# Chunk-sized loads in order of need, q over 128 partitions, and decay and bias vectors without element-sized transfers, in a linear-attention-then-highway kernel

## The chip, the cores and the metric

The kernel runs on one core of a Trainium2 chip. The core has five engines with queues of their own: TensorE (PE in the profile; its weight loads are PEld), VectorE (DVE), ScalarE (ACT), GpSimd (POOL) and SyncE (SP), and 16 DMA engines between the chip's memory (HBM), the on-chip memory (SBUF, 128 partitions) and back. Matmul results land in PSUM, which DVE and ACT read. The metric is the device time of one execution in microseconds (us); lower is better.

## The reference

For batch 4, 8 heads, 768 tokens and head dimension 64, a decayed linear attention runs over blocks of 64 tokens, and its output, with heads side by side as 512 features of 3072 tokens, goes through one highway layer:

```python
for b in range(nb):
    qb, kb, vb = (q[:, :, sl], k[:, :, sl], v[:, :, sl])
    intra = np.einsum('bhic,bhjc->bhij', qb, kb) * Dmask[None]      # lam ** (i - j), i >= j
    intra = np.einsum('bhij,bhjd->bhid', intra, vb)
    inter = np.einsum('bhid,bhde->bhie', qb * lam_pow[None], kv_state)
    out[:, :, sl] = intra + inter
    kv_state = lam_block * kv_state + np.einsum('bhsd,bhse->bhde', kb * rev_pow[None], vb)
...
H = np.maximum(x @ w_h, 0.0)
T = 1.0 / (1.0 + np.exp(-(x @ w_t + b_t)))
out = T * H + (1.0 - T) * x
```

lam holds one decay per head, b_t one bias per feature.

## The kernel before

**Tiling.** The kernel uses chunks of 128 tokens: 6 per batch, 24 in all, numbered n = 6 b + c. Heads go in four pairs (hp), so that two heads of 64 fill 128 partitions. The decay is split into a factor of the key's position, multiplied into v (scale_v, by pow_k), and one of the query's position, multiplied into the attention's output (by pow_q, in intra). Both come from lam by ln and exp on ACT at the start.

**One chunk.** cast_k and scale_v (POOL) turn the float32 loads of k and v into bf16; trans_k turns the chunk of k on PE, and ACT copies it out of PSUM. scores, inter and intra are the attention's matmuls, state adds to the running k-times-v sum, which ACT copies to SBUF for the next chunk. q is turned likewise: for batch 0 by chunk (load_q0, cast_q0, trans_q0), for batches 1 to 3 by head pair for a whole batch at once (load_q, cast_q, trans_q). There a partition takes J = 8 tokens that follow one another, so that 96 partitions hold the 768 tokens, and eight transposes of 96 columns give one head pair. All transposes use one PSUM buffer (tag "tr").

**The highway layer** goes in groups of four chunks (512 tokens). A unit (g, j) is ffn_h and ffn_t for 128 of the 512 features: four matmuls of 512 columns each, with relu and sigmoid behind. ffn_out adds T * (H - x) to x and turns it back on PE, one chunk at a time; ACT (at the end DVE too) copies it to o_sb, and SP stores it.

**What sets the order.** The schedule is manual: each engine runs its instructions in the order of the program. The main loop runs over i = 0 to 31. Iteration i casts chunk i+3 and one head pair of the next batch's q (c = 0 to 3) on POOL, turns k of chunk i+2, computes scores of chunk i+1 and the rest of chunk i, turns head pair c-1 of the next batch's q (c = 1 to 4), then does one ffn_h, one ffn_out and one ffn_t, where there is one. Units begin at i = 4, stores at i = 8; at i = 24 to 27 only units and stores are left, at i = 28 to 31 only stores.

**Loads.** All loads of q, k and v and all stores are issued by SP, in order. Batch 0 is loaded by chunk (256 KB each of k, q, v; line 61 and line 70); batches 1 to 3 by batch, 1.5 MB each of q (line 66), k and v (line 58), in that order. Batch 1 and 2's loads stand ahead of the first store, batch 3's behind the second. kf, vf and qf have two buffers of a whole batch each. lam is loaded three times by ACT's queue: once whole into every partition (line 76), and twice as every second element (lines 79, 80) for the head pairs; the bias is loaded with one element per partition (line 252). The weights are loaded and cast to bf16 by POOL's queue (lines 269, 270).

Of the kernel before, what the change touches and what calls it, by code (L numbers as in the profile page):

```python
# [16 lines left out]
def kernel(  # L17
# [11 lines left out]
    nc = tc.nc  # L29
    B, H, S, D = q.shape  # L30
    C = 128
    NCH = S // C
    NP = H // 2
    DM = H * D
    KC = DM // 128
    J = 8
    QP = S // J
    PP = C // J
    N = B * NCH
    G = 4  # L40
# [11 lines left out]
    def load_kv(b, what, src, cs=None):  # L52
        store = {"k": kf, "v": vf}[what]
        if b not in store:
            store[b] = load.tile([C, H, NCH, D], F32, tag=what + "f", name=f"{what}f{b}")
        t = store[b]
        if cs is None:
            nc.sync.dma_start(out=t.rearrange("p h c d -> p (h c) d"),
                              in_=src[b].rearrange("h (c p) d -> p (h c) d", p=C))
        else:  # L60
            nc.sync.dma_start(out=t[:, :, cs, :],
                              in_=src[b, :, cs * C:(cs + 1) * C, :].rearrange("h p d -> p h d"))

    def load_q(b):
        qf[b] = load.tile([QP, H, J * D], F32, tag="qf", name=f"qf{b}")
        nc.sync.dma_start(out=qf[b], in_=q[b].rearrange("h (p j) d -> p h (j d)", j=J))

    def load_q0(c):
        q0f[c] = load.tile([C, H, D], F32, tag="q0f", name=f"q0f{c}", bufs=3)
        nc.sync.dma_start(out=q0f[c], in_=q[0, :, c * C:(c + 1) * C, :].rearrange("h p d -> p h d"))  # L70

    load_kv(0, "k", k, 0)
    load_q0(0)
    load_kv(0, "v", v, 0)
# [6 lines left out]
    for c in range(1, 3):  # L81
        load_kv(0, "k", k, c)
        load_q0(c)
        load_kv(0, "v", v, c)
# [16 lines left out]
    nc.scalar.activation(ln_hp, lam_hp, AF.Ln)  # L101
# [22 lines left out]
    def cast_k(n, eng=None):  # L124
        b, c = divmod(n, NCH)
        kb[n] = work.tile([C, H, D], BF16, tag="kb", name="kb", bufs=4)
        (eng or nc.gpsimd).tensor_copy(kb[n], kf[b][:, :, c, :])  # L127

    def scale_v(n):
        b, c = divmod(n, NCH)  # L130
        vs[n] = work.tile([C, H, D], BF16, tag="vs", name="vs", bufs=4)
        nc.gpsimd.tensor_tensor(vs[n], in0=vf[b][:, :, c, :], in1=pow_k[:, :, c, :].to_broadcast([C, H, D]), op=ALU.mult)  # L132
# [4 lines left out]

    def trans_q0(c):
        if 0 not in qT:
            qT[0] = load.tile([128, NP, NCH, J * PP], BF16, tag="qT", name="qT0")  # L140
# [3 lines left out]
        nc.scalar.activation(qT[0][:, :, c, :], tr, AF.Copy)  # L144

    def cast_q(b, hp):
        qb[b, hp] = work.tile([QP, J, 2, D], BF16, tag="qb", name="qb")
        nc.gpsimd.tensor_copy(qb[b, hp].rearrange("p j e d -> p e j d"),  # L148
                              qf[b][:, 2 * hp:2 * hp + 2, :].rearrange("p e (j d) -> p e j d", j=J))

    def trans_q(b, hp):
        if hp == 0:
            qT[b] = load.tile([128, NP, NCH, J * PP], BF16, tag="qT", name=f"qT{b}")
        tr = ps.tile([128, J, QP], BF16, tag="tr", name="tr")
        for j in range(J):
            nc.tensor.transpose(tr[:, j, :], qb[b, hp][:, j], id128[0:QP, 0:QP])  # L156
        nc.scalar.activation(qT[b][:, hp].rearrange("p c (q j) -> p (c q) j", j=J),  # L157
                             tr.rearrange("p j q -> p q j"), AF.Copy)

    def trans_k(n):  # L160
# [6 lines left out]
    def scores(n):  # L167
        b, c = divmod(n, NCH)
        s_ps = ps.tile([C, 2, NP, C], F32, tag="s", name="s_ps")
        for hp in range(NP):  # L170
            for e in range(2):
                r = slice(64 * e, 64 * e + 64)
                nc.tensor.matmul(s_ps[:, e, hp, :], lhsT=kT[n][r, hp, :], rhs=qT[b][r, hp, c, :], start=True, stop=True)  # L173
        masked[n] = work.tile([C, 2, NP, C], BF16, tag="masked", name="masked")
        for e in range(2):
            nc.vector.tensor_tensor(masked[n][:, e], in0=s_ps[:, e],  # L176
                                    in1=tri.to_broadcast([C, NP, C]), op=ALU.mult)

    def inter(n):
        b, c = divmod(n, NCH)  # L180
        o_ps[n] = ps.tile([128, NP, C], F32, tag="o", name="o_ps")
        if c > 0:
            for hp in range(NP):
                nc.tensor.matmul(o_ps[n][:, hp, :], lhsT=s_bd[n % 2][:, hp, :], rhs=qT[b][:, hp, c, :],  # L184
                                 start=(hp == 0), stop=False, skip_group_check=True)

    def intra(n):
# [42 lines left out]
    def ffn_out(n, eng="act"):  # L230
        g, r = divmod(n, G)
        x_ps = ps.tile([C, DM], F32, tag="x", name="x_ps")
        for j in range(NP):
            for i, t in enumerate((xT[g], thmx[g])):
                nc.tensor.matmul(x_ps[:, j * 128:(j + 1) * 128], lhsT=t[:, j, r * C:(r + 1) * C], rhs=id128,  # L235
                                 start=(j == 0 and i == 0), stop=(i == 1), skip_group_check=True)
        o_sb = work.tile([C, DM], F32, tag="o_sb", name="o_sb", bufs=4)
        if eng == "act":
            nc.scalar.activation(o_sb, x_ps, AF.Copy)  # L239
# [13 lines left out]
    for c in range(3, NCH):  # L253
        load_kv(0, "k", k, c)
        load_q0(c)
        load_kv(0, "v", v, c)
# [21 lines left out]
    while i < N or units or outs:  # L278
        b, c = divmod(i, NCH)
        if i + 3 < N:  # L280
            cast_k(i + 3)
            scale_v(i + 3)
        if i + 3 < NCH:
            cast_q0(i + 3)
        if c < NP and b + 1 < B:
            cast_q(b + 1, c)
        if i + 2 < N:
            trans_k(i + 2)
        if i < N:
            inter(i)  # L290
        if i + 1 < N:
            scores(i + 1)
        if i < N:
            intra(i)
            state(i)
        if i + 2 < NCH:
            trans_q0(i + 2)
        if 1 <= c <= NP and b + 1 < B:
            trans_q(b + 1, c - 1)
        unit = units.pop(0) if units else None  # L300
        if unit:
            ffn_h(*unit)
        if outs:
            ffn_out(outs.pop(0), "dve" if i >= N and i % 2 else "act")
        if unit:
            ffn_t(*unit)
            if unit[1] == NP - 1:
                outs += range(unit[0] * G, unit[0] * G + G)
        if i < N and i % G == G - 1:
            units += [(i // G, j) for j in range(NP)]  # L310
        if c == 3 and b + 2 < B:
            load_q(b + 2)
            load_kv(b + 2, "k", k)
# [32 lines left out]
```

## Time and profile before

| what | value |
|---|---|
| median of 3 runs | 161.88 us (161.64 to 163.24) |
| the profiled execution's own time | 161.08 us |
| its span in the profile | 159.3 us |
| PE busy | 105.4 us, 66% |
| ACT, DVE busy | 77.2 us, 48%; 75.5 us, 47% |
| POOL busy | 57.1 us, 36% |
| moved by DMA | 26.41 MB, mean 166 GB/s |
| read from HBM, written to it | 20.98 MB, 6.29 MB |

A profile is of one execution: its span is 1.8 us shorter than that execution's time. "Busy" counts an engine's instructions, "idle before" the gap before an instruction with what ended it (`<-`). In a chain or timeline row the first number is the start in us from the span's beginning and the second the duration; in a row of stages each engine stands with its busy us and, in brackets, its instructions, and behind them the granted TensorE clock (1.00 is full), the mean share of the DMA engines in use and the rate that they moved. That share can pass 1, since packets overlap. Bytes moved are counted as written: the weights count as 1.05 MB although 2.1 MB are read. L148 is line 148 of the kernel before.

### The profile page before, as it was taken

Reading aid. Unit: us, or ns where it says so; the run is one execution under the profiler, and the core shown is the slowest. Engines: PE = TensorE matmul, PEld = TensorE weight load, DVE = VectorE, ACT = ScalarE, POOL = GpSimd, SP = SyncE. Lnnn points to the kernel's source line nnn. Section 1 sums busy time; section 2 is a strip of 40 time slices with the busy share of each in tenths; the row PEclk is TensorE's granted clock in tenths of the full one; section 3 lists DMA queues with packets and bytes.
Section 4 is the critical chain, followed back from the end, with each engine's and each line's share of the span. In section 5 each row is a group of like instructions: output and inputs, shape, how many; then the busy total and the mean of one; then the engine's idle time right before and its main releaser. Section 6 shows DMA issues by size and latency. Waiting matters only on the chain.

```text
span 159.3 us, 2882 instructions
## 1 busy us (share of the span) xinstructions
PE 105.4 (66%) x1127; PEld 69.3 (44%) x1144; DVE 75.5 (47%) x131; ACT 77.2 (48%) x140; POOL 57.1 (36%) x76
## 2 busy tenths in 40 slices
PE   0104661100275689999999989309999999999740
PEld 0103450000154464566666656205666666555440
DVE  4202333000040442998777778017568877856511
ACT  3065861100045448568885766044557676554320
POOL 4017722100594076784394097055244400000000
PEclk9999999999999999999999999955799999999985
DMA  4299999999999999999579999971111212313333
GB/s 88 47 197 222 190 194 234 218 226 222 205 220 219 184 240 214 221 220 218 126 192 229 205 217 198 219 285 48 66 66 66 70 66 88 114 68 132 127 142 132
DMA packets 36126, 26.41 MB, mean 166 GB/s; under 512 B 20496, under 2 KB 30736, under 8 KB 36112
## 3 DMA queue, kind: packets, MB, share of 16 engines
q1 hardware_dynamic: 33840, 25.17, 72.2%
q0 software_dynamic: 1056, 1.05, 3.9%
q8 instruction: 9, 0.15, 0.5%
q10 hardware_dynamic: 1216, 0.01, 0.4%
q14 instruction: 5, 0.04, 0.1%
HBM read 20.98 MB, written 6.29 MB: 171 GB/s over the span
## 4 chain that ended last, share of the span: by engine, by line
PE 45%; issue 18%; DMA 16%; POOL 7%; SPq 5%; ACT 5%; DVE 1%; POOLq 0%; ACTq 0%
PE h_ps L214 11%; PE t_ps L222 10%; DMA qf<-in_q_dram 7%; PE x_ps L235 6%; DMA out_dram<-o_sb 6%; PE o_ps L191 4%; SPq L70 4%; PE s_ps L173 3%; PE tr L156 3%; DMA vf<-in_v_dram 3%; PE kv_ps L205 3%; PE tr L163 3%; PE o_ps L184 2%; POOL vs L132 2%; POOL qb L148 2%
## 5 line engine op out<-in xcount | busy, mean ns | idle before, releaser
L176 DVE TENSOR_TENSOR masked<-s_ps,tri 128x512 bf16<-128x512 f32 x48 | 30.8, 682 | 41.4 <-PE s_ps L173 41.4
L132 POOL TENSOR_TENSOR vs<-vf,pow_k 128x512 bf16<-128x512 f32 x24 | 25.8, 1077 | 43.4 <-DMA vf<-in_v_dram 25.4
L214 PE MATMUL h_ps<-xT,wh 128*128 128x512 bf16 x87 | 25.4, 397 | 0.8 <-issue 0.4
L222 PE MATMUL t_ps<-xT,wt 128*128 128x512 bf16 x88 | 24.9, 396 | 0.3
L228 DVE TENSOR_TENSOR thmx<-t_sb,hmx 128x512 bf16<-128x512 bf16 x24 | 11.6, 484 | 28.3 <-ACT t_sb L225 28.0
L156 PE MATMUL tr<-id,qb 96*128 96x96 bf16 x96 | 7.6, 235 | 23.0 <-POOL qb L148 14.2
L225 ACT ACTIVATE t_sb<-t_ps,bt_col 128x512 bf16<-128x512 f32 x24 | 16.5, 687 | 12.1 <-PE t_ps L222 10.2
L239 ACT ACTIVATE o_sb<-x_ps 128x512 f32<-128x512 f32 x20 | 11.9, 597 | 20.6 <-PE x_ps L235 13.5
L209 ACT ACTIVATE s_bd<-kv_ps 64x256 bf16<-64x256 f32 x40 | 15.1, 377 | 10.9 <-PE kv_ps L205 10.1
L148 POOL CAST qb<-qf 96x1024 bf16<-96x1024 f32 x12 | 12.7, 1059 | 18.4 <-DMA qf<-in_q_dram 18.4
L157 ACT ACTIVATE qT<-tr 128x768 bf16<-128x768 bf16 x12 | 9.7, 810 | 16.3 <-PE tr L156 16.1
L217 DVE SCALAR_TENSOR_TENSOR hmx<-h_ps,xT 128x512 bf16<-128x512 f32 x24 | 16.4, 682 | 2.3 <-PE h_ps L214 2.2
L163 PE MATMUL tr<-id,kb 128*128 128x128 bf16 x96 | 11.0, 248 | 9.6 <-DVE kb L127 5.1
L156 PEld LDWEIGHTS <-qb 96*128 96x128 bf16 x96 | 6.2, 113 | 24.0 <-POOL qb L148 14.6
L127 POOL CAST kb<-kf 128x512 bf16<-128x512 f32 x23 | 14.0, 609 | 7.1 <-PE kv_ps L205 6.9
L196 DVE TENSOR_TENSOR xT<-o_ps,pow_q 128x512 bf16<-128x512 f32 x24 | 16.3, 679 | 0.0
L165 ACT ACTIVATE kT<-tr 128x512 bf16<-128x512 bf16 x24 | 14.1, 589 | 4.0 <-PE tr L163 4.0
L235 PE MATMUL x_ps<-id,xT 128*128 128x128 bf16 x96 | 14.0, 226 | 2.7 <-ACT o_sb L239 1.4
L163 PEld LDWEIGHTS <-kb 128*128 128x128 bf16 x96 | 8.3, 110 | 15.0 <-DVE kb L127 5.1
L235 PE MATMUL x_ps<-id,thmx 128*128 128x128 bf16 x96 | 14.3, 227 | 0.4 <-DVE thmx L228 0.4
L235 PEld LDWEIGHTS <-thmx 128*128 128x128 bf16 x96 | 9.7, 101 | 6.4 <-issue 3.4
L222 PEld LDWEIGHTS <-wt 128*128 128x128 bf16 x96 | 8.9, 102 | 7.6 <-issue 1.7
(41 smaller groups left out, 113.8 us busy)
## 6 DMA issues: line engine op xcount, KB each, us to landing
out_dram<-o_sb SPq DMA_DIRECT2D x24, 256.0 KB, 2.0
qf<-in_q_dram SPq DMA_DIRECT2D x3, 1536.0 KB, 11.3
kf<-in_k_dram SPq DMA_DIRECT2D x6, 256.0 KB, 5.3
q0f<-in_q_dram SPq DMA_DIRECT2D x6, 256.0 KB, 6.6
vf<-in_v_dram SPq DMA_DIRECT2D x6, 256.0 KB, 5.6
wh<-in_moe_w_h_dram POOLq DMA_DIRECT2D x1, 512.0 KB, 6.8
wt<-in_moe_w_t_dram POOLq DMA_DIRECT2D x1, 512.0 KB, 9.3
kf<-in_k_dram SPq DMA_DIRECT2D x3, 0.2 KB, 17.0
```

Of the source, the lines that this page charges most:

```text
L132: nc.gpsimd.tensor_tensor(vs[n], in0=vf[b][:, :, c, :], in1=pow_k[:, :, c, :].to_broadcast([C, H, D]), op=ALU.mult)
L148: nc.gpsimd.tensor_copy(qb[b, hp].rearrange("p j e d -> p e j d"), qf[b][:, 2 * hp:2 * hp + 2, :].rearrange("p e (j d) -> p e j d", j=J))
L156: nc.tensor.transpose(tr[:, j, :], qb[b, hp][:, j], id128[0:QP, 0:QP])
L163: nc.tensor.transpose(tr[:, hp, :], kb[n][:, 2 * hp:2 * hp + 2, :], id128)
L176: nc.vector.tensor_tensor(masked[n][:, e], in0=s_ps[:, e], in1=tri.to_broadcast([C, NP, C]), op=ALU.mult)
L196: nc.vector.tensor_tensor(xT[g][:, :, r * C:(r + 1) * C], in0=o_ps[n], in1=pow_q[:, :, c * C:(c + 1) * C], op=ALU.mult)
L209: nc.scalar.activation(s_bd[(n + 1) % 2][r, :, r], kv_ps[b][r, :, r], AF.Copy)
L214: nc.tensor.matmul(h_ps, lhsT=wh[:, kc, j * 128:(j + 1) * 128], rhs=xT[g][:, kc, :], start=(kc == 0), stop=(kc == KC - 1))
L217: nc.vector.scalar_tensor_tensor(hmx[g, j], in0=h_ps, scalar=0.0, in1=xT[g][:, j, :], op0=ALU.max, op1=ALU.subtract)
L222: nc.tensor.matmul(t_ps, lhsT=wt[:, kc, j * 128:(j + 1) * 128], rhs=xT[g][:, kc, :], start=(kc == 0), stop=(kc == KC - 1))
L225: nc.scalar.activation(t_sb, t_ps, AF.Sigmoid, bias=bt_col[:, j:j + 1])
L235: nc.tensor.matmul(x_ps[:, j * 128:(j + 1) * 128], lhsT=t[:, j, r * C:(r + 1) * C], rhs=id128, start=(j == 0 and i == 0), stop=(i == 1), s ...
```

## The change

k and v are loaded by chunk throughout, into eight buffers each (LA = 8). For batches 1 to 3, q is loaded by head pair (384 KB), into six buffers; a partition takes J = 6 tokens, so that all 128 partitions are used and six transposes of 128 columns make a head pair. One function, loads(n), issues all that belongs to chunk n: k, q of that chunk (batch 0 only), v, and one head pair of the next batch's q (c = 0 to 3). Chunks 0 to 7 are loaded ahead of the loop, and iteration i ends with loads(i + 8). lam is loaded once; its head-pair form is copied on ACT out of the logarithm that is there. The bias is loaded as four rows of 128 and turned by one transpose on PE. o_sb has six buffers in place of four.

```diff
-    J = 8
-    QP = S // J
-    PP = C // J
+    J = S // 128
+    LA = 8
...
+    def load_k(n):
+        b, c = divmod(n, NCH)
+        kf[n] = load.tile([C, H, D], F32, tag="kf", name="kf", bufs=LA)
+        nc.sync.dma_start(out=kf[n], in_=k[b, :, c * C:(c + 1) * C, :].rearrange("h p d -> p h d"))
...
-        qf[b] = load.tile([QP, H, J * D], F32, tag="qf", name=f"qf{b}")
-        nc.sync.dma_start(out=qf[b], in_=q[b].rearrange("h (p j) d -> p h (j d)", j=J))
+    def load_q(b, hp):
+        qf[b, hp] = load.tile([128, 2, J * D], F32, tag="qf", name="qf", bufs=6)
+        nc.sync.dma_start(out=qf[b, hp], in_=q[b, 2 * hp:2 * hp + 2].rearrange("e (p j) d -> p e (j d)", j=J))
...
+    def loads(n):
+        if n >= N:
+            return
+        b, c = divmod(n, NCH)
+        load_k(n)
+        if b == 0:
+            load_q0(c)
+        load_v(n)
+        if c < NP and b + 1 < B:
+            load_q(b + 1, c)
+
     lam_bc = singles.tile([128, H], F32)
     nc.scalar.dma_start(out=lam_bc, in_=lam.partition_broadcast(128))
-    lam_hp = singles.tile([128, NP], F32)
-    lam_v = lam.rearrange("(p two) -> two p", two=2)
-    nc.scalar.dma_start(out=lam_hp[0:64, :], in_=lam_v[0].partition_broadcast(64))
-    nc.scalar.dma_start(out=lam_hp[64:128, :], in_=lam_v[1].partition_broadcast(64))
...
+    bt_r = singles.tile([KC, 128], F32)
+    nc.scalar.dma_start(out=bt_r, in_=moe_b_t.rearrange("(j p) -> j p", p=128))
+    for n in range(4):
+        loads(n)
...
-    nc.scalar.activation(ln_hp, lam_hp, AF.Ln)
+    for e in range(2):
+        r = slice(64 * e, 64 * e + 64)
+        nc.scalar.activation(ln_hp[r, :], ln_bc[r].rearrange("p (hp e) -> p e hp", e=2)[:, e, :], AF.Copy)
...
-        qb[b, hp] = work.tile([QP, J, 2, D], BF16, tag="qb", name="qb")
+        qb[b, hp] = work.tile([128, J, 2, D], BF16, tag="qb", name="qb")
...
-        tr = ps.tile([128, J, QP], BF16, tag="tr", name="tr")
+        tr = ps.tile([128, J, 128], BF16, tag="tr", name="tr")
         for j in range(J):
-            nc.tensor.transpose(tr[:, j, :], qb[b, hp][:, j], id128[0:QP, 0:QP])
+            nc.tensor.transpose(tr[:, j, :], qb[b, hp][:, j], id128)
...
-        o_sb = work.tile([C, DM], F32, tag="o_sb", name="o_sb", bufs=4)
+        o_sb = work.tile([C, DM], F32, tag="o_sb", name="o_sb", bufs=6)
...
     scores(0)
+    id_f = singles.tile([KC, KC], F32)
+    nc.vector.tensor_copy(id_f, id128[0:KC, 0:KC])
+    bt_ps = ps.tile([128, KC], F32, tag="x", name="bt_ps")
+    nc.tensor.transpose(bt_ps, bt_r, id_f)
     bt_col = singles.tile([128, KC], F32)
-    nc.scalar.dma_start(out=bt_col, in_=moe_b_t.rearrange("(j p) -> p j", p=128))
...
-    load_q(1)
-    load_kv(1, "k", k)
-    load_kv(1, "v", v)
+    nc.vector.tensor_copy(bt_col, bt_ps)
+    for n in range(4, LA):
+        loads(n)
...
-        if c == 3 and b + 2 < B:
-            load_q(b + 2)
-            load_kv(b + 2, "k", k)
-            load_kv(b + 2, "v", v)
+        loads(i + LA)
```

SP's queue shows what the loads' new order is. In the kernel before, batch 0's last chunk is followed by the whole of batch 1 and then batch 2 (qf1 is q of batch 1, and so on; the number behind an underscore tells tiles of one name apart):

```order
L70 DMA q0f5_166<-in_q_dram 128x8x64
L61 DMA vf0_73<-in_v_dram 128x8x64
L66 DMA qf1_169<-in_q_dram 96x8x512
L58 DMA kf1_171<-in_k_dram 128x48x64
L58 DMA vf1_173<-in_v_dram 128x48x64
L66 DMA qf2_447<-in_q_dram 96x8x512
```

In the changed kernel, the first head pair of batch 1's q (qf_79) stands right behind the first chunk, and the second (qf_87) behind the second:

```order
L54 DMA kf_73<-in_k_dram 128x8x64
L67 DMA q0f_75<-in_q_dram 128x8x64
L59 DMA vf_77<-in_v_dram 128x8x64
L63 DMA qf_79<-in_q_dram 128x2x384
L54 DMA kf_81<-in_k_dram 128x8x64
L67 DMA q0f_83<-in_q_dram 128x8x64
L59 DMA vf_85<-in_v_dram 128x8x64
L63 DMA qf_87<-in_q_dram 128x2x384
```

So the q that iteration 0 casts moved from behind 18 loads to behind three.

Further on in SP's queue stand the stores. Before, two of them (o_sb_775, o_sb_858) come between batch 2's loads and batch 3's, and all others behind batch 3's:

```order
L58 DMA vf2_451<-in_v_dram 128x48x64
L242 DMA out_0_dram<-o_sb_775 128x512
L242 DMA out_0_dram<-o_sb_858 128x512
L66 DMA qf3_869<-in_q_dram 96x8x512
L58 DMA kf3_871<-in_k_dram 128x48x64
L58 DMA vf3_873<-in_v_dram 128x48x64
L242 DMA out_0_dram<-o_sb_944 128x512
```

In the changed kernel the first store (o_sb_829, of iteration 8) follows chunk 15's loads, and from there each of chunks 16 to 23 is loaded behind one store:

```order
L59 DMA vf_755<-in_v_dram 128x8x64
L63 DMA qf_757<-in_q_dram 128x2x384
L245 DMA out_0_dram<-o_sb_829 128x512
L54 DMA kf_841<-in_k_dram 128x8x64
L59 DMA vf_843<-in_v_dram 128x8x64
L245 DMA out_0_dram<-o_sb_914 128x512
L54 DMA kf_925<-in_k_dram 128x8x64
```

So eight stores now stand ahead of the last chunk's loads, where two stood ahead of the last batch's.

More of the change, by code (lines that the diff above doesn't have):

```diff
@@ L50 @@
     kf, vf, qf, q0f = {}, {}, {}, {}
[L52 to L62, printed above, removed]
@@ L64, in load_q, with load_v @@
-    def load_q(b):
-        qf[b] = load.tile([QP, H, J * D], F32, tag="qf", name=f"qf{b}")
-        nc.sync.dma_start(out=qf[b], in_=q[b].rearrange("h (p j) d -> p h (j d)", j=J))
+    def load_k(n):
+        b, c = divmod(n, NCH)
+        kf[n] = load.tile([C, H, D], F32, tag="kf", name="kf", bufs=LA)
+        nc.sync.dma_start(out=kf[n], in_=k[b, :, c * C:(c + 1) * C, :].rearrange("h p d -> p h d"))
+    def load_v(n):
+        b, c = divmod(n, NCH)
+        vf[n] = load.tile([C, H, D], F32, tag="vf", name="vf", bufs=LA)
+        nc.sync.dma_start(out=vf[n], in_=v[b, :, c * C:(c + 1) * C, :].rearrange("h p d -> p h d"))
@@ L68, in load_q0 @@
+    def load_q(b, hp):
+        qf[b, hp] = load.tile([128, 2, J * D], F32, tag="qf", name="qf", bufs=6)
+        nc.sync.dma_start(out=qf[b, hp], in_=q[b, 2 * hp:2 * hp + 2].rearrange("e (p j) d -> p e (j d)", j=J))
     def load_q0(c):
-        q0f[c] = load.tile([C, H, D], F32, tag="q0f", name=f"q0f{c}", bufs=3)
+        q0f[c] = load.tile([C, H, D], F32, tag="q0f", name="q0f", bufs=4)
         nc.sync.dma_start(out=q0f[c], in_=q[0, :, c * C:(c + 1) * C, :].rearrange("h p d -> p h d"))
-    load_kv(0, "k", k, 0)
@@ L73 @@
[L73 to L74 removed]
+    def loads(n):
+        if n >= N:
+            return
+        b, c = divmod(n, NCH)
+        load_k(n)
[4 more added lines that the diff above has]
+            load_q(b + 1, c)
     lam_bc = singles.tile([128, H], F32)
     nc.scalar.dma_start(out=lam_bc, in_=lam.partition_broadcast(128))
[L77 to L79 removed]
@@ L80 @@
-    nc.scalar.dma_start(out=lam_hp[64:128, :], in_=lam_v[1].partition_broadcast(64))
[L81 to L84, printed above, removed]
+    bt_r = singles.tile([KC, 128], F32)
+    nc.scalar.dma_start(out=bt_r, in_=moe_b_t.rearrange("(j p) -> j p", p=128))
+    for n in range(4):
+        loads(n)
     id128 = singles.tile([128, 128], BF16)
@@ L126, in cast_k @@
         kb[n] = work.tile([C, H, D], BF16, tag="kb", name="kb", bufs=4)
-        (eng or nc.gpsimd).tensor_copy(kb[n], kf[b][:, :, c, :])
+        (eng or nc.gpsimd).tensor_copy(kb[n], kf[n])
     def scale_v(n):
@@ L131, in scale_v @@
         vs[n] = work.tile([C, H, D], BF16, tag="vs", name="vs", bufs=4)
-        nc.gpsimd.tensor_tensor(vs[n], in0=vf[b][:, :, c, :], in1=pow_k[:, :, c, :].to_broadcast([C, H, D]), op=ALU.mult)
+        nc.gpsimd.tensor_tensor(vs[n], in0=vf[n], in1=pow_k[:, :, c, :].to_broadcast([C, H, D]), op=ALU.mult)
     def cast_q0(c, eng=None):
@@ L139, in trans_q0 @@
         if 0 not in qT:
-            qT[0] = load.tile([128, NP, NCH, J * PP], BF16, tag="qT", name="qT0")
+            qT[0] = load.tile([128, NP, S], BF16, tag="qT", name="qT0")
         tr = ps.tile([128, NP, C], BF16, tag="tr", name="tr")
@@ L143, in trans_q0 @@
             nc.tensor.transpose(tr[:, hp, :], qb[c][:, 2 * hp:2 * hp + 2, :], id128)
-        nc.scalar.activation(qT[0][:, :, c, :], tr, AF.Copy)
+        nc.scalar.activation(qT[0][:, :, c * C:(c + 1) * C], tr, AF.Copy)
     def cast_q(b, hp):
-        qb[b, hp] = work.tile([QP, J, 2, D], BF16, tag="qb", name="qb")
+        qb[b, hp] = work.tile([128, J, 2, D], BF16, tag="qb", name="qb")
         nc.gpsimd.tensor_copy(qb[b, hp].rearrange("p j e d -> p e j d"),
-                              qf[b][:, 2 * hp:2 * hp + 2, :].rearrange("p e (j d) -> p e j d", j=J))
+                              qf[b, hp].rearrange("p e (j d) -> p e j d", j=J))
     def trans_q(b, hp):
         if hp == 0:
-            qT[b] = load.tile([128, NP, NCH, J * PP], BF16, tag="qT", name=f"qT{b}")
-        tr = ps.tile([128, J, QP], BF16, tag="tr", name="tr")
+            qT[b] = load.tile([128, NP, S], BF16, tag="qT", name=f"qT{b}")
+        tr = ps.tile([128, J, 128], BF16, tag="tr", name="tr")
         for j in range(J):
-            nc.tensor.transpose(tr[:, j, :], qb[b, hp][:, j], id128[0:QP, 0:QP])
-        nc.scalar.activation(qT[b][:, hp].rearrange("p c (q j) -> p (c q) j", j=J),
+            nc.tensor.transpose(tr[:, j, :], qb[b, hp][:, j], id128)
+        nc.scalar.activation(qT[b][:, hp].rearrange("p (q j) -> p q j", j=J),
                              tr.rearrange("p j q -> p q j"), AF.Copy)
@@ L172, in scores @@
                 r = slice(64 * e, 64 * e + 64)
-                nc.tensor.matmul(s_ps[:, e, hp, :], lhsT=kT[n][r, hp, :], rhs=qT[b][r, hp, c, :], start=True, stop=True)
+                nc.tensor.matmul(s_ps[:, e, hp, :], lhsT=kT[n][r, hp, :], rhs=qT[b][r, hp, c * C:(c + 1) * C], start=True, stop=True)
         masked[n] = work.tile([C, 2, NP, C], BF16, tag="masked", name="masked")
@@ L183, in inter @@
             for hp in range(NP):
-                nc.tensor.matmul(o_ps[n][:, hp, :], lhsT=s_bd[n % 2][:, hp, :], rhs=qT[b][:, hp, c, :],
+                nc.tensor.matmul(o_ps[n][:, hp, :], lhsT=s_bd[n % 2][:, hp, :], rhs=qT[b][:, hp, c * C:(c + 1) * C],
                                  start=(hp == 0), stop=False, skip_group_check=True)
@@ L250 @@
     scores(0)
+    id_f = singles.tile([KC, KC], F32)
+    nc.vector.tensor_copy(id_f, id128[0:KC, 0:KC])
+    bt_ps = ps.tile([128, KC], F32, tag="x", name="bt_ps")
+    nc.tensor.transpose(bt_ps, bt_r, id_f)
     bt_col = singles.tile([128, KC], F32)
-    nc.scalar.dma_start(out=bt_col, in_=moe_b_t.rearrange("(j p) -> p j", p=128))
[L253 to L256, printed above, removed]
-    load_q(1)
-    load_kv(1, "k", k)
-    load_kv(1, "v", v)
+    nc.vector.tensor_copy(bt_col, bt_ps)
+    for n in range(4, LA):
+        loads(n)
     cast_k(1)
```

## The prediction

> **What bounds the kernel now.** I read the page first, then the waits, a table of stages, and the chain of waits. The page says that no engine is full over the whole span:
>
> ```profile
> PE 105.4 (66%) x1127; PEld 69.3 (44%) x1144; DVE 75.5 (47%) x131; ACT 77.2 (48%) x140; POOL 57.1 (36%) x76
> ```
>
> So the end is set by gaps. The waits (engine, line, what it waited for: us in total, times, longest) name the ones that end with a transfer:
>
> ```profile
> POOL vs L132 <- DMA vf<-in_v_dram: 25.4, 6, 7.2
> POOL qb L148 <- DMA qf<-in_q_dram: 18.4, 2, 13.0
> ACT o_sb L239 <- DMA out_dram<-o_sb: 7.1, 1, 7.1
> ACT ln_hp L101 <- DMA lam_hp<-in_lam_dram: 5.2, 1, 5.2
> ```
>
> The 13.0 us is a standstill, as the stages show:
>
> ```profile
> 2.00:3.00 1.00, 0.00 (x0) 0.00 (x0) 0.99 (x2) 0.41 (x1) 0.62 (x1) 1.00 0.57 124
> 5.00:6.00 1.00, 0.61 (x4) 0.34 (x4) 0.04 (x1) 0.00 (x0) 0.00 (x0) 1.00 0.16 26
> 7.00:8.00 1.00, 0.00 (x0) 0.10 (x1) 0.43 (x1) 0.00 (x0) 0.00 (x0) 1.00 0.08 8
> ...
> 10.00:30.00 20.00, 8.44 (x80) 5.66 (x79) 5.06 (x8) 11.23 (x22) 9.29 (x12) 1.00 1.27 211
> ...
> 30.00:40.00 10.00, 0.00 (x0) 0.00 (x0) 0.00 (x0) 0.00 (x0) 0.00 (x0) 1.00 1.15 222
> 40.00:70.00 30.00, 22.04 (x228) 15.09 (x230) 12.75 (x22) 14.06 (x25) 18.20 (x22) 1.00 1.09 215
> ...
> 100.00:110.00 10.00, 3.19 (x33) 1.98 (x31) 2.92 (x4) 3.10 (x6) 4.41 (x5) 0.65 0.77 209
> ```
>
> From 30 to 40 us nothing computes while the DMA engines move 222 GB/s. At 5 to 8 us they nearly stand still, though loads are queued: the element-sized lam transfers are running there, and SP's next load takes 5.09 us to issue. The rate is otherwise near 211 to 222 GB/s, with chunk-sized loads (10 to 30 us) as with batch-sized ones (40 to 70 us). The chain (start, duration) shows the same places:
>
> ```profile
> 4.41 5.09 SPq L70
> ...
> 28.61 13.02 issue
> 41.65 1.05 POOL qb L148
> 42.75 0.84 PE tr L156 x8
> ...
> 48.68 0.81 PE tr L156 x8
> ...
> 59.84 1.49 PE h_ps L214 x3
> ...
> 74.14 4.11 issue
> ...
> 80.22 11.31 DMA qf<-in_q_dram
> ...
> 95.72 10.03 DMA out_dram<-o_sb
> ```
>
> Transfers hold the end until about 107 us; from there the loads are in, and PE works off the backlog. So a faster kernel needs work to start sooner, not a faster transfer.
>
> **The change, part by part.** *When iteration 1 can turn q.* I call the first matmul of ffn_h in iteration i h(i). Sizes and durations:
>
> ```profile
> qf<-in_q_dram SPq DMA_DIRECT2D x3, 1536.0 KB, 11.3
> kf<-in_k_dram SPq DMA_DIRECT2D x6, 256.0 KB, 5.3
> ...
> wh<-in_moe_w_h_dram POOLq DMA_DIRECT2D x1, 512.0 KB, 6.8
> ```
> ```profile
> 4.62 0.43 DVE L127 CAST kb<-kf 128x512 bf16<-128x512 f32 x1
> ```
> ```profile
> L132 POOL TENSOR_TENSOR vs<-vf,pow_k 128x512 bf16<-128x512 f32 x24 | 25.8, 1077 | 43.4 <-DMA vf<-in_v_dram 25.4
> L148 POOL CAST qb<-qf 96x1024 bf16<-96x1024 f32 x12 | 12.7, 1059 | 18.4 <-DMA qf<-in_q_dram 18.4
> ```
>
> Data start at about 2.4 us (124 GB/s in a stage whose successors at full rate give 215). The first k, 262 KB or 1.2 us of that rate, is in use at 4.62, so a load lands about 1 us behind its last byte. Before cast_q of iteration 0, POOL must take chunk 3's v and q. Ahead of that in the queues stand 12 loads of 256 KB, three q parts of 384 KB (a quarter of 1536), and both weights, 512 KB each: 5248 KB, 5.37 MB, 25.0 us at 215 GB/s. So chunk 3 is in at 28.4. POOL adds 1.08 for v, about 0.6 for the chunk's q and about 0.8 for qb (1.059 by 768 elements over 1024; if time goes by instruction, 1.06), and trans_q starts near 31.0 in place of 42.75. That is 11.7 us. If the early transfers keep the holes of 5 to 8 us, it is 4 us less: the stages there miss some 0.8 MB. Nothing in the changed queues is element-sized any more, so I take the full rate.
>
> *From there to h(8).* Between 42.75 and 59.84 the chain goes from q's transposes to k's, the attention, and through ACT's copies to the next transposes, 5.9 us each time (42.75 to 48.68), with no transfer in it. It stays: 17.1 us, so h(4) is at 48.1. Chunk 5, needed at 42.8, has 7.3 MB ahead of and with it: in at 37.5, cast by 40. From h(4) to h(8), 59.84 to 73.65, it is PE's work: 13.8, so h(8) at 61.9.
>
> ```profile
> 73.65 1.03 PE L214 MATMUL h_ps<-xT,wh 128*128 128x512 bf16 x4
> ...
> 130.79 0.39 PE L163 MATMUL tr<-id,kb 128*128 128x128 bf16 x4
> ...
> 132.24 1.03 PE L214 MATMUL h_ps<-xT,wh 128*128 128x512 bf16 x4
> ```
>
> *From h(8) to h(21).* Before, 58.6 us, with the three waits at 74, 80 and 95 us in it. PE's own work is:
>
> ```profile
> 114.39 0.34 PE tr L156 x8
> ...
> 128.78 0.86 PE h_ps L214 x4
> ...
> 131.18 0.22 PE o_ps L184 x4
> ...
> 132.08 0.33 PE kv_ps L205 x4
> 132.41 0.86 PE h_ps L214 x4
> ```
>
> An iteration without q's transposes is 3.63 (128.78 to 132.41); seven of the 13 have them, 0.34 each; a batch's first chunk lacks the 0.22, its last the 0.33, twice each. 13 x 3.63 + 2.4 - 1.1 = 48.5. So h(21) is at 110.4 if loads keep ahead.
>
> *Do they?* The last k needed at h(21) is chunk 23's. All of q, k and v (18432 KB), the weights and eight stores, less the last v, are 21248 KB, 21.76 MB: at 215 GB/s 101.2 us, landed at 104.6, cast at 105.2. It is needed 1.45 us before h(21) (130.79 to 132.24), at 108.9. The cover is 3.7 us, and it is gone at 207 GB/s. So the waits at 74 and 80 us go, and what is late next is PE itself. SP isn't held: by the same sum it comes to the first store at about 71 us, some 5 us ahead of chunk 15's landing, when o_sb of iteration 8 (about 63.5) is long there. That store then lands near 77; its buffer is wanted again six stores later, at 85.7, so the wait at 95 us goes too. With eight k and v buffers, chunk n's load waits for chunk n-8 to be cast, three iterations before it is issued by the program; q's seventh part waits for the cast near 31, and SP is there at about 40.
>
> *The rest.* From h(21) to the end (159.3) is 27.1 us, unchanged. Six transposes of 128 columns for eight of 96 (0.84 slow, 0.34 fast) save between nothing and a quarter each; three lie in the slow chain: -0.5. POOL's cast is off the path. The two small ACT copies of ln_hp cost some 0.4 us where 5.2 us of waiting goes, both before the first v is ready. The bias costs one transpose on PE and two small copies on DVE, behind scores(0); masked(1) is queued behind them. Nearest rows: nothing to 0.7 us, hidden, since chunk 2's load is what PE waits for there. If the bias rows were late, that queue would slip, but they are the second transfer on ACT's queue.
>
> Sum: 31.0 + 17.1 + 13.8 + 48.5 + 27.1 - 0.5 = 137.0 span. The profiled execution took 1.8 more than its span (161.08 to 159.3): 138.8. The median of the runs is 0.8 above that execution: **139.5 us**.
>
> The Trainium skill's page "DMA: Bandwidth & Descriptors" speaks against the change: its "Rules for kernel authors" ask for 1 MiB or more per transfer, and its fit in "Anatomy of one DMA" (2.0 us plus bytes over 436 GB/s) would give 256 KB a rate near 100 GB/s alone, an estimate by that page. The stages with 211 and 215 GB/s do not bear it out as long as several loads are in flight.
>
> **The rivals.**
>
> *Transfers set the pace.* With stores and 256-byte pieces mixed throughout, the rate may fall below 207; the stage at 100 us shows 209. At 200 GB/s chunk 23's k lands at 112.2 and h(21) is 2.05 later (0.6 for the cast, 1.45 on PE): 114.3 + 27.1 + 1.8 + 0.8 = 144; at 190, 150. For it: before, long stretches were never mixed like this. Against it: chunk loads beside the weights ran at 211, batch loads at 215, and the stages show no other loss.
>
> *Faster.* If PE's slow chain from 31 to 48 us runs quicker since work is denser there, the end falls to the transfers' own line: 104.6 + 2.05 + 29.7 = 136; at the 222 GB/s of the stage at 30 us about 133, and a last load that lands 1 us sooner makes it 132.
>
> *Slower, by the clock.* Nothing gets late but PE pauses for chunks in each iteration, and its clock drops:
>
> ```profile
> 110.90 1.71 PE t_ps L222 x4
> ...
> 126.47 0.86 PE t_ps L222 x4
> ```
>
> After the idle stretch at 100 us the granted clock was 0.65, and four matmuls took 1.71 in place of 0.86. An iteration at that speed is about 7.1, 3.4 more. All 13 slow: 184 us. It decides from 6.6 slow iterations on, where the gain of 22 us is used up. Against it: by the sum above PE has no long gap left from h(4) on. The Trainium skill's "TensorE: Matmul & The Clock Gate", Part 1, halves the clock after an idle window of about 3.4 us; by that rule the pauses that the sum leaves are too short.
>
> *Slower, by the loads' size.* A load takes 5.3 us to land; 215 GB/s needs 4.3 of 256 KB in flight. If only three are, 148 GB/s: chunk 23 at 150.4, an end near 182. It decides below about 170 GB/s (chunk 23's k landed at 130). That is where the skill's rule on sizes would lead.
>
> *The change doesn't do it:* q is there early, but POOL or PE is held at chunk 3 to 5 by another load until 42 us, and the later waits come back in other places; the time stays near 161. For it speaks only that vs waits for vf for 25.4 us in all; against it, that chunk 3's v now has 5.37 MB ahead of it.
>
> **How the numbers follow.** Forecast 0.58; transfers set the pace 0.24; faster 0.10; slow clock 0.03; small loads 0.03; nothing gained 0.02. The range from 132 (the faster case's end) to 150 (transfers at 190 GB/s) holds most of the first three, and takes in the 4 us of the early holes and the bounds of the small edits. Faster by over 1% is 0.92, within 1% (about what a measurement can tell) 0.02, slower 0.06.
>
> **What would show it.** In the changed profile: no wait of qb on qf and no stage without PE work after 15 us; the first trans_q at 31, h(4) near 48, h(8) near 62, h(21) near 110; the DMA rate near 215 without a hole from 3 to 104 us, then stores only; the iterations from 8 on at 3.6 to 4.0 us each with PE full. Wrong would be vs still waiting for vf late in the run (transfers set the pace), h(4) later than 52 (the early rate), granted clock under 1 between 50 and 110 us, or ACT waiting for o_sb's store.

## The result, and the profile after

The changed kernel takes 137.67 us (median of 5 runs, 137.32 to 139.28) against 161.88 us before; the ratio is 0.851, with a 95% interval of 0.845 to 0.858. The forecast was 139.5. All medians in this document leave out disturbed runs, of which e2, e5, e6, e8 and e9 had one each (e5's took 170 us and e6's 213), and the traces of e5 and e8 are of such runs. The profile of the changed kernel is of its slowest execution, 139.28 us, 2.9 us longer than its span; the execution of 137.67 us has a span of 135.5 us.

The page of the changed kernel, its span and its engines:

```profile
span 136.4 us, 2889 instructions
...
PE 102.3 (75%) x1105; PEld 68.1 (50%) x1121; DVE 74.1 (54%) x133; ACT 77.6 (57%) x141; POOL 54.7 (40%) x76
```

PE's work is nearly what it was (105.4 us before); some 20 of the 23 us of span that went were PE's gaps. Of the waits of the engines, these two are the large ones that end with a transfer:

```profile
POOL vs L135 <- DMA vf<-in_v_dram: 12.2, 7, 4.8
...
POOL kb L130 <- DMA kf<-in_k_dram: 11.7, 6, 7.0
```

No wait of the q cast on q's load is left (18.4 us before), and none of ACT on a store (7.1 before). The stages, with the moved GB/s in the last column:

```profile
2.00:10.00 8.00, 1.80 (x16) 1.21 (x16) 3.16 (x8) 5.48 (x12) 2.01 (x3) 1.00 1.12 225
10.00:30.00 20.00, 7.55 (x69) 5.02 (x70) 4.94 (x10) 7.50 (x14) 8.97 (x13) 1.00 1.20 233
30.00:40.00 10.00, 6.68 (x68) 5.11 (x67) 2.29 (x4) 4.51 (x8) 6.45 (x10) 1.00 0.96 208
40.00:70.00 30.00, 27.33 (x308) 18.51 (x310) 20.57 (x37) 20.77 (x37) 18.66 (x23) 1.00 1.09 234
70.00:100.00 30.00, 29.68 (x358) 19.78 (x363) 22.61 (x41) 22.41 (x42) 15.65 (x20) 1.00 0.98 237
100.00:105.00 5.00, 4.95 (x70) 3.35 (x69) 3.62 (x8) 3.63 (x8) 1.63 (x2) 1.00 0.25 92
```

The hole at 5 to 8 us is gone (225 GB/s from 2 to 10), PE works where nothing did from 30 to 40 us, and it is full from 70 us on: 29.68 of 30. At 100 us the loads are over and only stores run. The timeline of PE gives the marks of the prediction: q's first transposes, h(4), h(8) and h(21). (Of the first of these groups of ffn_h three of four matmuls are recorded.)

```profile
30.40 0.80 PE L159 MATMUL tr<-id,qb 128*128 128x128 bf16 x6 [0.69 <-ACT qT L147]
...
47.43 0.83 PE L217 MATMUL h_ps<-xT,wh 128*128 128x512 bf16 x3 [0.22 <-issue]
...
60.58 1.03 PE L217 MATMUL h_ps<-xT,wh 128*128 128x512 bf16 x3
...
108.80 1.03 PE L217 MATMUL h_ps<-xT,wh 128*128 128x512 bf16 x4
```

The chain of waits shows what holds the start now:

```profile
13.99 11.19 DMA kf<-in_k_dram
25.23 0.61 POOL kb L130
...
29.05 0.68 POOL qb L151
```

Chunk 3's k takes 11.2 us from issue to landing. The weights' two loads were issued at 13 us and share the way; e7 shows that they are the cause.

### The profile page after: what moved, and what is told of

It is laid out like the page before. It is cut to its first block, busy times and chain, and to the rows that moved or that the text cites. A ratio compares the mean times of both kernels' runs of the same rounds, so it can differ in the third digit from the quotient of the medians.

```text
span 136.4 us, 2889 instructions
## 1 busy us (share of the span) xinstructions
PE 102.3 (75%) x1105; PEld 68.1 (50%) x1121; DVE 74.1 (54%) x133; ACT 77.6 (57%) x141; POOL 54.7 (40%) x76
## 3 DMA queue, kind: packets, MB, share of 16 engines
q0 software_dynamic: 1056, 1.05, 4.7%
## 4 chain that ended last, share of the span: by engine, by line
PE 55%; SPq 9%; DMA 8%; POOL 7%; issue 7%; DVE 6%; ACT 4%; POOLq 0%; DVEq 0%
PE h_ps L217 13%; PE t_ps L225 13%; PE x_ps L238 9%; DMA kf<-in_k_dram 8%; PE o_ps L194 4%; PE s_ps L176 4%; SPq L59 4%; PE kv_ps L208 3%; PE o_ps L187 3%; PE tr L166 3%; DVE masked L179 3%; PE tr L159 3%; POOL vs L135 2%; POOL kb L130 2%; SPq L63 2%
## 5 line engine op out<-in xcount | busy, mean ns | idle before, releaser
L217 PE MATMUL h_ps<-xT,wh 128*128 128x512 bf16 x85 | 24.0, 380 | 0.7 <-issue 0.2
L225 PE MATMUL t_ps<-xT,wt 128*128 128x512 bf16 x91 | 24.2, 379 | 0.2
L130 POOL CAST kb<-kf 128x512 bf16<-128x512 f32 x23 | 14.1, 615 | 23.5 <-DMA kf<-in_k_dram 11.7
L231 DVE TENSOR_TENSOR thmx<-t_sb,hmx 128x512 bf16<-128x512 bf16 x24 | 10.3, 430 | 20.2 <-ACT t_sb L228 20.0
L217 PEld LDWEIGHTS <-wh 128*128 128x128 bf16 x96 | 8.5, 99 | 7.1 <-issue 0.3
L176 PE MATMUL s_ps<-qT,kT 64*128 64x128 bf16 x192 | 10.8, 240 | 0.7 <-ACT qT L147 0.7
L194 PE MATMUL o_ps<-masked,vs 128*64 128x128 bf16 x192 | 11.1, 243 | 0.0
```

The lines of the kernel that those rows point to most:

```text
L130: (eng or nc.gpsimd).tensor_copy(kb[n], kf[n])
L194: nc.tensor.matmul(o_ps[n][64 * e:64 * e + 64, hp, :], lhsT=vs[n][:, 2 * hp + e, :], rhs=masked[n][:, e, hp, :], start=(hp == 0 and c == 0 ...
L217: nc.tensor.matmul(h_ps, lhsT=wh[:, kc, j * 128:(j + 1) * 128], rhs=xT[g][:, kc, :], start=(kc == 0), stop=(kc == KC - 1))
L225: nc.tensor.matmul(t_ps, lhsT=wt[:, kc, j * 128:(j + 1) * 128], rhs=xT[g][:, kc, :], start=(kc == 0), stop=(kc == KC - 1))
```

## The experiments

The theory: the end is the time of q's first transposes, plus a slow chain of 17 us, plus PE's own work. Loads count only up to the start of that chain; afterwards they have slack. The main rival was that the transfers set the pace throughout.

**e1, the kernel before with only the lam and bias loads changed.**

```diff
-    nc.scalar.dma_start(out=lam_hp[0:64, :], in_=lam_v[0].partition_broadcast(64))
-    nc.scalar.dma_start(out=lam_hp[64:128, :], in_=lam_v[1].partition_broadcast(64))
...
+    nc.scalar.dma_start(out=bt_r, in_=moe_b_t.rearrange("(j p) -> j p", p=128))
...
-    nc.scalar.activation(ln_hp, lam_hp, AF.Ln)
+    for e in range(2):
...
+        nc.scalar.activation(ln_hp[r, :], ln_bc[r].rearrange("p (hp e) -> p e hp", e=2)[:, e, :], AF.Copy)
...
+    nc.tensor.transpose(bt_ps, bt_r, id_f)
...
-    nc.scalar.dma_start(out=bt_col, in_=moe_b_t.rearrange("(j p) -> p j", p=128))
+    nc.vector.tensor_copy(bt_col, bt_ps)
```

> The kernel before with only the lam and bias loads changed. Theory (the element-sized loads cost the early transfers 0.8 MB, about 4 us, and everything behind waits for transfers): q of batch 1 lands up to 4 us sooner than 41.65 us, and the time is about 158 us (157 to 159.5). Rival (the hole is made good later, since loads run ahead anyway): 161.9 us, no change.

Measured: 158.14 us against 161.27 for the kernel before beside it, ratio 0.978 (0.970 to 0.986). In its stages the hole is filled:

```profile
4.00:9.00 5.00, 1.29 (x12) 0.96 (x14) 1.02 (x3) 4.14 (x10) 1.49 (x2) 1.00 1.29 223
```

The cast of batch 1's q starts at 37.8 us in place of 41.65. So these few kilobytes cost some 3 us, about what the theory has.

**e2, the changed kernel with the element-sized loads put back** (e1's edit, the other way).

> The changed kernel with the element-sized lam and bias loads put back. Theory: chunk 3 lands up to 4 us later, the first transposes of batch 1's q with it, and nothing later makes it good, since PE is the bound: about 141 us (139.5 to 142). Rival (the slack of the transfers absorbs it): 137.7.

Measured: 141.95 us, 4.3 more than the changed kernel's median, at the upper end of the range. A stage and PE's timeline:

```profile
2.00:10.00 8.00, 0.61 (x4) 0.45 (x5) 2.81 (x7) 1.49 (x2) 0.62 (x1) 1.00 0.56 131
```
```profile
34.15 0.80 PE L159 MATMUL tr<-id,qb 128*128 128x128 bf16 x6 [0.69 <-ACT qT L147]
```

131 GB/s in place of 225 over the first 8 us is 0.75 MB, and q's first transposes are 3.75 us later. Nothing made that good: the slack of the later transfers is of no use to the start.

**e3, q's parts behind the batch's last chunk:** order undone, sizes kept.

```diff
-        if c < NP and b + 1 < B:
-            load_q(b + 1, c)
+        if c == NCH - 1 and b + 1 < B:
+            for hp in range(NP):
+                load_q(b + 1, hp)
```

> The changed kernel with the next batch's four q parts loaded behind the last chunk of a batch in place of one with each chunk: order undone, sizes kept. Theory (the size counts more than the place: the first part of 384 KB then lands at about 30 us, since chunks 1 to 5 and it are 6.2 MB with the weights): the first transposes of q at about 32 in place of 30.4, 139.3 us (138 to 141). Rival (the order is the gain): most of the standstill of 13 us comes back, 147 to 150.

Measured: 140.57 us. PE's timeline, and stages around the four q parts:

```profile
32.58 0.82 PE L160 MATMUL tr<-id,qb 128*128 128x128 bf16 x6 [6.71 <-POOL qb L152]
```
```profile
28.00:30.00 2.00, 0.00 (x0) 0.00 (x0) 0.00 (x0) 0.00 (x0) 0.00 (x0) 1.00 1.20 219
30.00:32.00 2.00, 0.00 (x0) 0.00 (x0) 0.00 (x0) 0.00 (x0) 0.30 (x1) 1.00 0.99 343
32.00:34.00 2.00, 0.82 (x6) 0.66 (x7) 0.00 (x0) 0.56 (x1) 2.00 (x3) 1.00 1.04 338
```

PE waits 6.71 us for q, but the first transposes are only 2.2 us later, and the time 2.9. So the place of the parts is worth 3 us, and most of the standstill of 13 us stays away without it. In e3 the first transposes are still 10.2 us sooner than in the kernel before; 3.75 of these are the element-sized loads' (e2), and 1.1 are the shape of q's load (33.71 in e9). The 5.3 that are left agree with what the rest of a 1.5 MB load of q would add (1.18 MB at 222 GB/s, an estimate), but no run puts that load back. The stages hold something I had not expected: with q's parts the rate jumps from 219 to about 340 GB/s. e9 comes back to it.

**e4, k and v of batches 1 to 3 by batch:** sizes undone, q as changed.

```diff
-        load_k(n)
         if b == 0:
+            load_k(n)
             load_q0(c)
-        load_v(n)
+            load_v(n)
+        elif c == 0:
+            ...  # k and v of the whole batch, 1.5 MB each, two buffers each
```

> The changed kernel with k and v of batches 1 to 3 loaded by batch, 1.5 MB each, at the place of the batch's first chunk: sizes undone, q as changed. Theory: the first v of batch 1 lands behind 10.5 MB, near 52 us, POOL's queue waits for it with q's fourth part behind, and the first ffn_h comes near 55 in place of 47: 145.5 us (142 to 149); the rate falls from 235 to about 215 GB/s while batch-sized loads run. Rival (same bytes in nearly the same order): 138.

Measured: 146.24 us, 8.6 more than the changed kernel. POOL's timeline, and PE's for h(4):

```profile
43.20 0.61 POOL L137 CAST kb<-kw 128x512 bf16<-128x512 f32 x1 [4.72 <-DMA kw<-in_k_dram]
50.22 1.06 POOL L142 TENSOR_TENSOR vs<-vw,pow_k 128x512 bf16<-128x512 f32 x1 [6.41 <-DMA vw<-in_v_dram]
51.22 0.82 POOL L158 CAST qb<-qf 128x768 bf16<-128x768 f32 x1
```
```profile
53.14 1.49 PE L224 MATMUL h_ps<-xT,wh 128*128 128x512 bf16 x3 [0.22 <-issue]
```

v is used at 50.2, with q's fourth part queued behind it in POOL's queue, and h(4) follows at 53.1 (forecast 55, against 47.4 in the changed kernel); time and step agree with the forecast. The expected fall of the rate was not clear: the 10 us stages from 30 to 50 us moved 220 and 228 GB/s, against 208 and 263 in the changed kernel.

**e5, without the loads of v for chunks 12 to 23**, k standing in for them.

```diff
-        load_v(n)
+        if n < 12:
+            load_v(n)
+        else:
+            vf[n] = kf[n]
```

> The changed kernel without the loads of v for chunks 12 to 23 (v's place is taken by k, so that part of the output is of other data): 3.1 MB less to load. Theory (PE is the bound from the first ffn_h on, the transfers have slack): no change, 137.7 us (137 to 138.5). Rival (transfers set the pace of the second half): 13 us less to move, 126 to 133.

Measured: 137.3 us. With 3.1 MB less to move the time stays, though part of the output is then of other data: in the second half the transfers are not the bound. This is the run that decides between the theory and its main rival.

**e6, PE kept busy in its waits of iterations 0 to 3.**

```diff
+    def warm(m):
+        junk = ps.tile([128, GT], F32, tag="h", name="junk")
+        for _ in range(m):
+            nc.tensor.matmul(junk[:, 0:C], lhsT=id128, rhs=id128, start=True, stop=True)
...
             trans_q0(i + 2)
+            warm(40 if i == 0 else 5)
         if 1 <= c <= NP and b + 1 < B:
             trans_q(b + 1, c - 1)
+            if i < G - 1:
+                warm(6)
```

> The changed kernel with matmuls of the identity by itself put on PE where it waits in iterations 0 to 3 (40 in iteration 0, then 5 and 6 an iteration), results unused. It measures the slow chain from 30 to 47 us. Theory (PE's low clock makes that chain 5.9 us an iteration; with the clock up it is about 4.2, until chunk 5's landing near 37 holds it): 133 us (131.5 to 135.5). Rival (the chain is ACT's and the loads', or the clock doesn't come up): 137.5 to 140, since the added matmuls only cost.

Measured: 134.4 us, 3.3 less than the changed kernel. PE's timeline:

```profile
30.76 0.80 PE L159 MATMUL tr<-id,qb 128*128 128x128 bf16 x6 [0.15 <-ACT qT L147]
35.85 0.49 PE L159 MATMUL tr<-id,qb 128*128 128x128 bf16 x6 [1.00 <-ACT qT L147]
40.40 0.49 PE L159 MATMUL tr<-id,qb 128*128 128x128 bf16 x6 [1.05 <-ACT qT L147]
43.24 0.50 PE L159 MATMUL tr<-id,qb 128*128 128x128 bf16 x6
43.58 1.03 PE L217 MATMUL h_ps<-xT,wh 128*128 128x512 bf16 x4
```

Useless matmuls made the kernel faster: six transposes take 0.49 us in place of 0.80, an iteration of the chain 4.6 to 5.1 in place of 5.9, and h(4) is at 43.6 in place of 47.4. So part of the 17 us is that PE runs at a slower pace behind its pauses. The column of the granted clock doesn't show this: from 30 to 40 us it reads 1.00 in the changed kernel, and 0.85 here, where PE is the faster:

```profile
30.00:40.00 10.00, 7.38 (x104) 6.08 (x103) 3.67 (x6) 5.77 (x11) 7.80 (x12) 0.85 1.11 234
```

So PE's pace is read from the durations. The forecast 4.2 an iteration was too low: ACT's copies in that chain (0.8 for q, 0.6 and 0.8 for the others) do not get shorter. The Trainium skill's "TensorE: Matmul & The Clock Gate", Part 1, has the clock rise after a busy window of about 3.4 us and fall after an idle one; the change from 0.80 to 0.49 agrees with it. The first transposes, at 30.76, are still slow in spite of the 40 matmuls in iteration 0, behind which PE waits 2.7 us for chunk 3; how long a pause slows PE down, no run here shows.

**e7, the weight loads issued behind iteration 0's casts.**

```diff
-    nc.gpsimd.dma_start(out=wh, ...)
-    nc.gpsimd.dma_start(out=wt, ...)
...
             cast_q(b + 1, c)
+        if i == 0:
+            nc.gpsimd.dma_start(out=wh, ...)
+            nc.gpsimd.dma_start(out=wt, ...)
```

> The changed kernel with the two weight loads issued behind iteration 0's casts in place of ahead of chunk 2's. Theory (until 28 us the loads are the bound, and the weights' 1.05 MB stand ahead of chunk 3): the first transposes of batch 1's q come 4 to 4.5 us sooner, 133.5 us (132.5 to 135). Rival (PE's and POOL's own chain is the bound there): 137.7.

Measured: 135.15 us. PE's timeline, and POOL's for chunk 3's v, first in the changed kernel and then here:

```profile
24.21 0.80 PE L159 MATMUL tr<-id,qb 128*128 128x128 bf16 x6 [0.69 <-ACT qT L147]
30.15 0.80 PE L159 MATMUL tr<-id,qb 128*128 128x128 bf16 x6 [1.12 <-ACT qT L147]
38.49 0.80 PE L159 MATMUL tr<-id,qb 128*128 128x128 bf16 x6 [0.69 <-POOL kb L130]
...
43.27 1.91 PE L217 MATMUL h_ps<-xT,wh 128*128 128x512 bf16 x4
```
```profile
27.44 1.06 POOL L135 TENSOR_TENSOR vs<-vf,pow_k 128x512 bf16<-128x512 f32 x1 [1.60 <-DMA vf<-in_v_dram]
```
```profile
21.25 1.06 POOL L135 TENSOR_TENSOR vs<-vf,pow_k 128x512 bf16<-128x512 f32 x1 [1.73 <-DMA vf<-in_v_dram]
```

Chunk 3's v and the first transposes come 6.2 us sooner, more than expected. But the weights now stand ahead of chunk 5, and the third transposes wait for POOL: the step from 30.15 is 8.3 us in place of 5.9. So the loads do bound the start, and moving bytes only moves the wait; 2.5 us remain. That loads count only up to the start of the chain is true of the changed kernel's order, and not once a load that the chain needs is pushed back, here as in e4.

**e8, q on 96 partitions with eight tokens each again.**

```diff
-    J = S // 128
+    J = 8
+    QP = S // J
...
-        qf[b, hp] = load.tile([128, 2, J * D], F32, tag="qf", name="qf", bufs=6)
+        qf[b, hp] = load.tile([QP, 2, J * D], F32, tag="qf", name="qf", bufs=6)
...
```

> The changed kernel with q on 96 partitions with eight tokens each again. Theory: POOL's cast and PE's transposes of q are a little longer, off the path but for three turns of the slow chain: 138.1 us (137.5 to 138.8). Rival (128 partitions are part of the gain, by the load's rate or POOL's cast): 140 or more.

Measured: 140.06 us, ratio to the kernel before 0.868 (0.859 to 0.877), 2.4 us more than the changed kernel. The theory fails here: the spread of q over 128 partitions is worth 2.4 us, not 0.5. POOL's timeline, for chunk 3's v, has the loss already:

```profile
29.52 1.06 POOL L136 TENSOR_TENSOR vs<-vf,pow_k 128x512 bf16<-128x512 f32 x1 [2.62 <-DMA vf<-in_v_dram]
```

That is 2.1 us later than in the changed kernel, at the end of a wait for a transfer, before POOL has cast or PE turned any part of batch 1's q. So the longer cast and the two more transposes aren't behind these 2.1 us.

**e9, e3 and e8 together**, to see four q parts of either shape by themselves.

> The changed kernel with both the q parts behind each batch's last chunk and q on 96 partitions with eight tokens each; to be held against e3, where the four q parts on 128 partitions ran by themselves at 338 to 343 GB/s between 30 and 34 us. Theory (the shape of q's load sets its rate: 96 partitions by 2 KB move at about 215 GB/s, as q did in the kernel before): the stage of the four q parts runs at 205 to 225, the first qb comes about 1 us later and the fourth 2.7 us later than in e3, 142 to 143 us. Rival (e8 lost its time on POOL's longer cast and PE's two more transposes): the stage stays above 300 GB/s, and the time 141 us.

Measured: 141.42 us, 0.9 more than e3. The stages that answer to e3's:

```profile
28.00:30.00 2.00, 0.00 (x0) 0.00 (x0) 0.00 (x0) 0.00 (x0) 0.00 (x0) 1.00 1.27 242
30.00:32.00 2.00, 0.00 (x0) 0.00 (x0) 0.00 (x0) 0.00 (x0) 0.00 (x0) 1.00 1.07 238
32.00:34.00 2.00, 0.29 (x4) 0.29 (x5) 0.00 (x0) 0.00 (x0) 1.39 (x2) 1.00 1.06 249
```

The same bytes at the same place run at 238 to 249 GB/s to 96 partitions, and at 338 to 343 to 128. The rate itself is above the 205 to 225 expected, but far from the rival's 300. So the shape of q's load sets its rate. The first qb starts 0.9 us later than in e3, as expected, the fourth 1.6 in place of 2.7; the time lies between the two forecasts, and POOL's four casts are 0.2 longer each, so it doesn't decide by itself. The rate and e8's chunk 3 do. By an estimate from the two rates, the three parts ahead of chunk 3 (1.18 MB) take 1.4 us more to 96 partitions, of e8's 2.1. Why 96 partitions with pieces of 2 KB are slower, no run here shows.

**e10, e6 and e7 together:** 16 matmuls in iteration 0, then 6 and 6, and the weights behind iteration 1's casts.

> e6 and e7 together: PE kept busy in its waits of iterations 0 to 3 (16 matmuls in iteration 0, then 6 and 6), and the weight loads issued behind iteration 1's casts. Theory (the two costs lie one behind the other in the start, and PE bounds the rest): the first ffn_h at 39 to 41 us in place of 47.4, 130.5 us (129 to 133). Rival (with the start shorter the last loads become the bound, or the weights now come too late for the first ffn_h): 133.5 to 136.

Measured: 132.91 us, ratio to the kernel before 0.825 (0.820 to 0.829): the fastest version here. PE's and POOL's timelines (POOL's row is the cast of chunk 7's k):

```profile
39.83 1.88 PE L217 MATMUL h_ps<-xT,wh 128*128 128x512 bf16 x4
...
55.60 1.03 PE L217 MATMUL h_ps<-xT,wh 128*128 128x512 bf16 x4
...
103.81 1.03 PE L217 MATMUL h_ps<-xT,wh 128*128 128x512 bf16 x4
```
```profile
41.25 0.61 POOL L130 CAST kb<-kf 128x512 bf16<-128x512 f32 x1 [4.93 <-DMA kf<-in_k_dram]
```

h(4) is at 39.8, some 7 us sooner than in the changed kernel (where three of the four matmuls of h(4) are recorded), of which 4.8 reach the end. From h(4) to h(8) it takes 15.8 us in place of 13.2 or a little more: chunk 7 now lands behind the weights, and the first ffn_h is at the slow pace (1.88 for four matmuls). From h(8) to h(21) it is 48.2 us, the same as in the changed kernel: PE's own work, even with everything 5 us sooner. e6 and e7 have 48.2 there too.

**e11, four o_sb buffers again.**

```diff
-        o_sb = work.tile([C, DM], F32, tag="o_sb", name="o_sb", bufs=6)
+        o_sb = work.tile([C, DM], F32, tag="o_sb", name="o_sb", bufs=4)
```

> The changed kernel with four o_sb buffers again. Theory (a store lands some 5 us after its issue, and by the sums on record four buffers leave about 1 us): no change, 137.7 us (137 to 139). Rival (the two more buffers are what ended ACT's wait of 7.1 us for a store): 140 to 145.

Measured: 137.69 us, no change. Its trace has no wait of ACT for a store either, so the 7.1 us didn't go with the buffers; that they went with the loads' new order is what is left, and no run undoes that alone.

## Why the prediction was right

| mark | forecast, us | measured, us |
|---|---|---|
| q's first transposes | 31.0 | 30.4 |
| h(4) | 47.6 with the -0.5 | 47.4, first recorded |
| h(8) | 61.4 | 60.6 |
| h(8) to h(21) | 48.5 | 48.2 |
| h(21) to the end | 27.1 | 27.6 |
| span | 137.0 | 136.4 |

The marks are of the slowest of five executions. The median came out 1.8 us under the forecast, 1.5 of it because the span of the median execution is 135.5 and not 137.0; the step from span to median was put at 2.6 (1.8 and 0.8), and is 2.2 for that execution.

**When iteration 1 can turn q** held: bytes ahead of chunk 3 over the rate. That it held to 0.6 us is in part luck, since three errors of size met in it. Without the weights chunk 3's v is taken up at 21.25 (e7), where the sum's own working gives 23.5: the rate was about 240 GB/s and not 215. The weights then cost 6.2 us (e7), where their 1.05 MB were put at 4.9. And with q cast at 29.8, the first transposes waited until 30.4 for ACT's copy of the q transposed before them out of the one transpose buffer (the row at 30.40), which the sum did not have. The picture was off too: the weights held chunk 3's k for 11.2 us, so that PE stood still from the last work on chunk 2 to 25.9, where I had written that no stage after 15 us would be without PE work.

**The hole of the element-sized loads** was put at 4 us: 3.1 alone (e1), 4.3 the other way (e2).

**From there to h(8)** held, and e6 shows what it consists of: the chain is as slow as the kernel before had it because PE runs at its slower pace there. The rival "faster" was a real possibility, but the change alone did not bring it about; it took added work on PE. Transposes of 128 columns saved nothing in the slow chain (0.80 for six, 0.81 to 0.84 for eight before), where I had put up to a quarter.

**From h(8) to h(21), and do loads keep ahead:** PE was the bound, by e5 and by the 48.2 us of e6, e7 and e10. The working of the cover was off twice, in opposite ways. The rate of 235 in place of 215 is the term that was mis-sized: loads ended before 100 us in place of 104.6. And SP *was* held, for free q buffers from 41 us on and by stores from 68 us on, as the changed kernel's own waits of SP say:

```profile
SPq L63 <- POOL kb L130: 5.1, 4, 2.9
SPq L245 <- ACT kT L168: 4.6, 3, 2.1
```

The stores held it for some 11 us in all before the last load is issued, at 91 us, and it cost nothing, since the loads had the slack. The dip to 208 GB/s from 30 to 40 us lies before these waits, behind one of 1.0 us; what made it, no run shows.

**Six transposes for eight, and q on 128 partitions,** is where a step failed: I costed it by POOL and PE and called the rate of loads the same for all shapes. e8 puts 2.4 us on it, and e9 shows that it is the load's rate. It is inside the better rate above.

**Transfers set the pace** (0.24) didn't come: e5. Nor did PE slow down later: its iterations from h(8) to h(21) took 3.4 to 4.0 us each. (The stages quoted above read a granted clock of 1.00 to 105 us, but by e6 that column doesn't settle it.) The rule of large transfers in the Trainium skill's "DMA: Bandwidth & Descriptors", "Rules for kernel authors", did not decide, and the fit quoted with it is the page's for transfers that GpSimd issues, where these are SP's: 66 loads of 256 and 384 KB ran at 225 to 237 GB/s in most stages with several in flight, 27 larger and smaller ones at 211 to 222 before, and e4's 1.5 MB loads lost 8.6 us by what had to wait behind them.

Of the 24 us, undoing one part at a time gives back 4.3 (element-sized loads), 8.6 (size of k and v), 2.9 (place of q) and 2.4 (shape of q): 18 together, though parts need not add up. The rest is not shown singly; splitting q's 1.5 MB load into parts, which none of these undoes, is the likely holder, since without it the first cast would wait for 1.2 MB more; that is worked out under e3, and not shown by a run.

## What to carry to other kernels

Find the first piece of work that waits, count the bytes that stand ahead of it in all queues, weights included, and divide by the rate that the stages show: that gave the start within 1 us here, with errors in the rate and in the weights' share that cancelled. Then see from the trace whether the rest is an engine's own work; if so, a shorter start goes through to the end as far as it makes no later load late, and further gains in loading do not. What a load costs depends on its shape as well as its size, so a stage in which that load runs by itself is worth looking for before calling its rate the usual one.

## What the runs showed that I had not expected

The same 1.5 MB of q moved at about 340 GB/s in pieces of 1536 bytes to 128 partitions, and at about 240 in pieces of 2 KB to 96. k, q0 and v in pieces of 256 bytes moved at about 220 just ahead of them (e3). And in a stage bound by a chain of short dependent steps, 67 unused matmuls on PE saved 3.3 us (e6), while the granted clock's column read 1.00 in the slower kernel.
